# Attention and two MoE layers on one core: the first expert's rows earlier, scatters side by side, new planner prices, another overflow path

## The chip, the cores and the metric

The kernel is one program on one core of a Trainium2 chip. The metric is the device time of one execution in microseconds (us). The engines are TensorE (PE; its weight loads are PEld), VectorE (DVE), ScalarE (ACT), GpSimd (POOL) and SyncE (SP), which here only issues DMAs.

## The reference

Windowed attention with a distance bias on 4 x 8 heads of 576 positions, a dense layer of 2304 tokens through 2048 units, and a layer of eight experts of 1024 units, where each token goes to the expert whose embedding is nearest to it.

```python
scores = scale * q @ k.T + bias            # 128-wide causal window
x = softmax(scores) @ v                    # as 2304 tokens x 512
h = x @ w_in
x = (h - tanh(h)) @ w_out
logits = normed(x) @ normed(expert_emb).T / tau
idx = argmax(logits); gate = softmax(logits)[idx]
for e in range(8):
    mask = idx == e
    out[mask] = gate[mask] * (relu(x[mask] @ w1[e]) @ w2[e])
```

## The kernel before, in words

Tokens run in nine groups of 256 (`NG`), two blocks of 128 each. For a block, `quarter` makes the attention (scores on PE, the bias and the minimum on DVE, the exponential on ACT, a split into high and low parts on ACT and POOL or DVE, a turn by DMA, the product on PE), and `x_out` turns the result into `xT`. For a group, `step` runs eight times (`p` counts steps): the product `h` at L710, tanh on ACT (L715), a subtraction (L718), the high part `gh` (L723, ACT) and the low part `gl` (L727, DVE), and the product `acc` at L734. Every fp32 product is made of three products of such parts. Group 0 is visited twice, with half of the weights each time and group 1 in between.

After its last step `route` takes a group's 256 tokens to the experts: norms, three bfloat16 parts of each row (L806, L810), logits (L819; for the last group L833), the choice (`chain`), the place in the expert's list (`slot`), the gate, and two scatters of 128 rows into `bucket` in DRAM (L890, an indirect DMA of POOL). `emb` makes the normed embeddings `enT` and `en3` (load `ec` at L278, transposes at L293); it borrows the buffers `gh1` and `gl1`. It stands in the loop over visits outside the test for a first visit.

After group 6 `choose` ranks the experts by their counts so far; expert 0 of the second layer is the largest of these. `space` reads the counts again after group 7 and moves that expert's later rows up to row 256 where it has fewer, so that its first two tiles need no row of the last group. `settle` ranks the others after the last group and gives them capacities (`CAPS`, 384 down to 256). `e_rows` fetches a tile of an expert's rows (L1103, a turning DMA, or L1088, a plain one with transposes on PE; `side` at L1108 for gate and token), adds the parts (L1120) and splits the sum into `xA` or `xT` (L1127, L1130). `e_weight` loads weights (L1059, L1061) and splits them (L1065, L1069). `expert` makes `he` (L1169), `ge` (L1185, L1191), `y` (L1200, L1204), scales by the gate (L1225 or L1223) and `put` scatters 128 rows into the output (L1229). The third tile of expert 0 goes through `turned`. At the end `overflow` would take the rows past an expert's capacity: a branch on all engines (L1466) with a loop in it.

The order of all work is made by `Plan.order`: a list of tasks with engines and their costs, due times, what they read and write. It picks the task that can start first, then the one due first. `late` and `lag` are added to the time at which a result counts as there; `port=True` says that the task, on DVE, can't begin while POOL runs; `SW` is POOL's DMA queue. The engines run in the order so made.

## Time and profile before

| | |
|---|---|
| median of 3 runs | 804.57 us (803.22 to 805.38) |
| profiled execution, its own time | 803.59 us |
| its span, first to last instruction | 801.9 us |
| PE busy | 766.4 us (96%) |
| DVE, ACT, POOL busy | 576.8, 424.9, 344.1 us |
| granted TensorE clock, mean | 0.987 |
| moved by DMA | 124.29 MB, 155 GB/s on average |

The profile comes from one execution. Busy time is that of the engine's own instructions; register, branch, semaphore and DMA-issuing instructions don't count. A matmul at a lower granted clock is busy for longer.

### The profile page before, as it was taken

The numbers are of one execution on the slowest core, as the hardware profiler recorded it, in microseconds if no ns is written. First come the engines' busy times: TensorE is split into PE (matmuls) and PEld (weight loads), VectorE is DVE, ScalarE is ACT, GpSimd is POOL, SyncE is SP. The second block draws the span as 40 slices with busy tenths as digits, with TensorE's granted clock in tenths as the row PEclk, the third lists the DMA queues.
The fourth block names the chain that finished last, engine by engine and source line by source line (L and its number), as shares of the span: only waits on it lengthen the run. The fifth ranks groups of instructions, "written<-read, shape, count | busy, mean of one in ns | idle before, by whom it ended". The sixth has DMA issues, their size and how long they took to land.

```text
span 801.9 us, 15261 instructions
## 1 busy us (share of the span) xinstructions
PE 766.4 (96%) x5193; PEld 678.1 (85%) x5193; DVE 576.8 (72%) x1501; ACT 424.9 (53%) x963; POOL 344.1 (43%) x339
## 2 busy tenths in 40 slices
PE   6998999799999999999999999998999999979995
PEld 4877899689898999989989998987889889869894
DVE  4798898688687687698887875978449877657420
ACT  4776876545665464555645642654145655545220
POOL 3233225765564155253644721655124644632210
PEclk9999999899999999999999999999999999999998
DMA  9983389936455264454364425681366988975100
GB/s 322 407 328 112 80 258 281 208 101 135 99 117 143 72 120 101 109 131 115 74 146 113 92 66 125 198 222 42 112 178 198 254 233 214 245 179 175 37 29 30
DMA packets 152472, 124.29 MB, mean 155 GB/s; under 512 B 115309, under 2 KB 119405, under 8 KB 152128
## 3 DMA queue, kind: packets, MB, share of 16 engines
q1 hardware_dynamic: 149360, 111.40, 52.3%
q0 software_dynamic: 3024, 11.82, 4.3%
q8 instruction: 42, 0.69, 0.4%
q14 instruction: 46, 0.38, 0.2%
HBM read 84.30 MB, written 22.06 MB: 133 GB/s over the span
## 4 chain that ended last, share of the span: by engine, by line
PE 74%; DVE 8%; issue 6%; DMA 4%; POOL 3%; ACT 2%; SPq 2%; POOLq 0%; ACTq 0%; DVEq 0%
PE h L710 21%; PE acc L734 20%; PE he L1169 9%; PE y L1204 8%; PE o L571 3%; PE sc L489 3%; PE y L1200 2%; PE of L560 2%; PE sc L483 1%; DMA est<-in_w 1%; SPq L1103 1%; DVE xf L1120 1%; PE misc L546 1%; DMA out<-yo,ix 1%; PE misc L662 1%
## 5 line engine op out<-in xcount | busy, mean ns | idle before, releaser
L710 PE MATMUL h<-xT,wi 128*128 128x256 f32 x1728 | 227.2, 284 | 3.0 <-DVE wi L349 1.6
L710 PEld LDWEIGHTS h<-xT,wi 128*128 128x128 f32 x1728 | 217.7, 191 | 10.1 <-DVE wi L349 2.2
L734 PE MATMUL acc<-wo,gh 128*128 128x512 f32 x576 | 184.9, 402 | 1.2 <-ACT gh L723 1.2
L734 PEld LDWEIGHTS acc<-wo,gh 128*128 128x128 f32 x576 | 101.3, 191 | 17.3 <-ACT gh L723 1.6
L734 PE MATMUL acc<-wo,gl 128*128 128x512 f32 x288 | 113.6, 395 | 0.5 <-DVE gl L727 0.5
L1204 PE MATMUL y<-eo,ge 128*128 128x512 f32 x336 | 88.5, 397 | 4.3 <-DVE ge L1191 2.9
L715 ACT ACTIVATE t<-h 128x512 f32<-128x512 f32 x72 | 43.0, 597 | 84.5 <-PE h L710 83.4
L525 ACT ACTIVATE p<-sc,mx 128x256 f32<-128x256 f32 (+1 forms) x128 | 59.3, 465 | 48.4 <-DVE mx L511 31.5
L1204 PEld LDWEIGHTS y<-eo,ge 128*128 128x128 f32 x336 | 59.6, 188 | 16.3 <-DVE ge L1191 4.7
L511 DVE CUSTOM_DVE_ANT_0 sc<-sc,bias 128x256 f32<-128x256 f32 (+1 forms) x136 | 49.9, 375 | 27.9 <-PE sc L489 19.7
L727 DVE TENSOR_TENSOR gl<-t,gh 128x512 fp32r<-128x512 f32 x72 | 62.3, 866 | 5.7 <-ACT gh L723 4.9
L734 PEld LDWEIGHTS acc<-wo,gl 128*128 128x128 f32 x288 | 54.8, 190 | 13.3 <-DVE gl L727 0.9
L383 POOL TENSOR_TENSOR khl<-stk,khl 64x512 fp32r<-64x512 f32 x25 | 34.4, 1378 | 62.3 <-ACT khl L379 40.8
L1229 POOL DMA_INDIRECT out<-yo,ix x23 | 24.1, 1047 | 86.2 <-ACT yo L1225 57.8
L535 POOL TENSOR_TENSOR ph<-p,ph 128x512 f16<-128x512 f32 (+1 forms) x32 | 38.9, 1216 | 50.8 <-ACT ph L530 35.1
L1191 DVE SCALAR_TENSOR_TENSOR ge<-he,ge 128x256 fp32r<-128x256 f32 x104 | 28.6, 313 | 39.8 <-ACT ge L1185 39.5
L1169 PEld LDWEIGHTS he<-xA,ei 128*128 128x128 f32 x384 | 54.4, 188 | 2.7
L1169 PE MATMUL he<-xA,ei 128*128 128x288 f32 (+2 forms) x384 | 56.5, 295 | 0.0
L1169 PEld LDWEIGHTS he<-xT,ei 128*128 128x128 f32 x384 | 54.5, 192 | 2.2
L1169 PE MATMUL he<-xT,ei 128*128 128x288 f32 (+2 forms) x384 | 55.9, 298 | 0.0
L718 DVE TENSOR_TENSOR t<-h,t 128x512 f32<-128x512 f32 x72 | 49.3, 685 | 7.2 <-ACT t L715 6.9
L723 ACT CAST gh<-t 128x512 fp32r<-128x512 f32 x72 | 44.6, 619 | 16.9 <-DVE t L718 13.3
(223 smaller groups left out, 1416.7 us busy)
## 6 DMA issues: line engine op xcount, KB each, us to landing
est<-in_w SPq DMA_DIRECT2D x128, 256.0 KB
bucket<-in_c_pad SPq DMA_DIRECT2D x8, 1155.0 KB
rawi<-in_w_in SPq DMA_DIRECT2D x16, 511.8 KB
rawo<-in_w_out SPq DMA_DIRECT2D x16, 511.8 KB
stk<-in_k SPq DMA_DIRECT2D x30, 256.0 KB
stq<-in_q SPq DMA_DIRECT2D x28, 256.0 KB
vst<-in_v SPq DMA_DIRECT2D x30, 128.0 KB
xe<-bucket SPq DMA_DIRECT2D x3, 384.0 KB
```

What stands on the lines that cost most here:

```text
L383: self.eng(e).tensor_tensor(out=k, in0=r4("k")[64:128], in1=k.bitcast(F32), op=ALU.subtract)
L511: nc.vector.tensor_tensor_reduce(out=x, in0=x, in1=self.bias[:, h, c0:c1], scale=-0.125, scalar=mx[:, 1:2] if m else 3.0e38, op0=ALU.add, ...
L525: nc.scalar.activation(out=v["p32"][:, jj * W:(jj + 1) * W], in_=x, func=AF.Exp, scale=-1.0, bias=v["mx"][jj][:, 0:1], accum_out=self.sums ...
L535: self.eng(e).tensor_tensor(out=ph[:, 2 * W:4 * W], in0=v["p32"][:, 0:2 * W], in1=ph[:, 0:2 * W], op=ALU.subtract)
L710: nc.tensor.matmul(h3(v["h"], f2), lhsT=w[:, a, k, :], rhs=xT[c][:, :, k, :], start=(k == 0 and n == 0), stop=(k == KD - 1 and n == 2))
L715: nc.scalar.activation(out=v["t"], in_=v["h"].rearrange("p a b -> p (a b)"), func=AF.Tanh)
L718: nc.vector.tensor_tensor(out=v["t"], in0=v["h"].rearrange("p a b -> p (a b)"), in1=v["t"], op=ALU.subtract)
L723: nc.scalar.copy(out=v["gh"], in_=v["t"])
L727: self.eng(e).tensor_tensor(out=v["gl"], in0=v["t"], in1=v["gh"].bitcast(F32), op=ALU.subtract)
L734: nc.tensor.matmul(self.acc[g, t], lhsT=v[a][:, c0:c0 + 128], rhs=self.w["o", fs[f2]][:, c, :], start=(first and f2 == 0 and n == 0), stop ...
L1169: nc.tensor.matmul(h[:, 0:N], lhsT=w[:, a, c0:c0 + 128], rhs=xT()[b][:, k, 0:N], start=(k == 0 and n == 0), stop=(k == KD - 1 and n == 2))
L1204: nc.tensor.matmul(y[t], lhsT=gt(f, a)[:, (t - ts[0]) * 128:(t - ts[0] + 1) * 128], rhs=self.w["o", f0 + f][:, b, :], start=(f == 0 and n ...
```

## The change

- `emb` is called on the first visit of group 0 only.
- `space` runs after group 6, beside `choose`, instead of after group 7. The first two tiles of expert 0 (`soon`) depend on the scatters of groups 0 to 6, and are due ten steps ahead of the expert instead of four.
- The two scatters of a group no longer wait for each other; each follows the two of the group before (the first group's all pads), and the loads of rows follow the last two that were sent. A small memset on POOL stands ahead of the second one. The scatters into the output no longer wait for each other.
- The planner counts the results of the loads of keys, queries, values and expert weights 1.2 us later (`lag=LAG`; one of five places is shown below), takes a scatter to occupy its queue for 1.06 us, and marks some 25 more tasks with `port=True` (three are shown): the low parts of weights, the splits of the probabilities, the row parts, the choice, place, gate and ranking, `keep`, and the sums of the rows.
- The overflow path is written without POOL's DMAs: rows come by SP, and go out through DRAM row by row. A branch hint for POOL is set ahead of it, `nt` holds the counts too.

```diff
+LAG = 1.2
+SOON = 10
...
     def order(self, places):
...
             elif e == "SW":
-                free["POOL"] = max(free.get("POOL", 0.0), st) + 1.04
-                free[e] = st + eng[e]
-                end = st + eng[e] + 2.0
+                free["POOL"] = max(free.get("POOL", 0.0), st) + 1.06
+                free[e] = st + 1.06
+                end = st + eng[e] + 1.5
...
-            lat = self.LAT.get(e, 0.05) + late
+            lat = self.LAT.get(e, 0.05) + late + lag
...
-        self.nt = self.cst.tile([1, 2 * E + 1], I32, name="nt")
+        self.nt = self.cst.tile([1, 3 * E + 1], I32, name="nt")
...
-        P.add(LOENG, lo, due, r=[wf, (key, 0), "at"], w=[(key, 1)])
+        P.add(LOENG, lo, due, r=[wf, (key, 0), "at"], w=[(key, 1)], port=True)
...
-            P.add({"SP": 0.73}, lambda e: load("k"), due - 2, r=["at"], w=[k, "stk"])
+            P.add({"SP": 0.73}, lambda e: load("k"), due - 2, r=["at"], w=[k, "stk"], lag=LAG)
...
         def scatter(t):
-            nc.gpsimd.indirect_dma_start(
+            if t:
+                nc.gpsimd.memset(r["sm"][:, 0, 7:8], 0.0)
+            x = nc.gpsimd.indirect_dma_start(
                 out=self.bucket, out_offset=bass.IndirectOffsetOnAxis(ap=r["ix"][:, t:t + 1].bitcast(U32), axis=0),
-                in_=self.xrow[t], in_offset=None)
+                in_=self.xrow[t], in_offset=None).ins
+            if t:
+                self.tc.declare_no_dep(x, self.sent[-1], reason="each row of the bucket is written once")
+            n = 2 if g != N0 else len(self.sent) - t
+            self.follow(x, self.sent[len(self.sent) - t - n:len(self.sent) - t])
+            self.sent.append(x)
...
-                  r=["ix", "x2g"] + [("x3", t, n) for n in range(3)] + [("pad", n) for n in range(E)], w=["bucket"])
-        P.add({"DVE": 0.4}, cums, due, r=["oh", "small"], w=["cum"])
+                  r=["ix", "x2g"] + [("x3", t, n) for n in range(3)] + [("pad", n) for n in range(E)], w=[("bk", g, t)])
+        P.add({"DVE": 0.4}, cums, due, r=["oh", "small"], w=["cum"], port=True)
+
+    def follow(self, x, insts):
+
+        info = mybir.DependencyInfo(mybir.DependencyClass.Sync, mybir.DependencyReason.DATA)
+        for y in insts:
+            self.tc.add_manual_dep(x, y.name, info, reason="rows of the bucket")
...
-            nc.sync.dma_start_transpose(out=x.rearrange("p n k t -> p (n k) t")[:, :, 0:w], in_=rows)
+            self.follow(nc.sync.dma_start_transpose(out=x.rearrange("p n k t -> p (n k) t")[:, :, 0:w], in_=rows).ins, self.sent[-2:])
...
+        rows = [("bk", g, n) for g in range(NG - 2 if v["soon"] else NG) for n in range(2)]
...
-            P.add({"SP": 2.2}, turn, due - 6, r=["at", "bucket", ("place", c)], w=[x], late=LATE)
+            P.add({"SP": 2.2}, turn, due - 6, r=["at", ("place", c)] + rows, w=[x], late=LATE)
...
-        P.add(add, lambda e: join(e, 1), due, r=[x], w=["xf"])
+        P.add(add, lambda e: join(e, 1), due, r=[x], w=["xf"], port=True)
...
         def put(_, t):
             n = T if short(t) else 128
-            nc.gpsimd.indirect_dma_start(
+            x = nc.gpsimd.indirect_dma_start(
                 out=self.out, out_offset=bass.IndirectOffsetOnAxis(ap=v["ix", t][0:n].bitcast(U32), axis=0),
-                in_=v["yo", t][0:n], in_offset=None, bounds_check=NT - 1, oob_is_err=False)
+                in_=v["yo", t][0:n], in_offset=None, bounds_check=NT - 1, oob_is_err=False).ins
+            for y in self.puts:
+                self.tc.declare_no_dep(x, y, reason="each row of the result is written once")
+            self.puts.append(x)
...
-                if b == 0:
-                    self.emb(P, 0)
+                    if b == 0:
+                        self.emb(P, 0)
...
                 if g == NG - 3:
                     self.choose(P, p + 2)
+                    self.space(P, p + 2)
...
-                self.e_rows(P, v, t, d - 4 + t)
+                self.e_rows(P, v, t, d - (SOON if n == 0 else 4) + t)
             self.expert(P, v, d, n == len(passes) - 1, n == 1)
             if n == 0:
-                self.space(P, due - 6)
                 tail()
...
     def overflow(self):
...
-        load = lambda j: nc.values_load(self.nt[0:1, j:j + 1], min_val=0, max_val=self.NOV * (E if j == E else 1))
-        with tc.If(load(E) > 0):
+        load = lambda j, lo, hi: nc.values_load(self.nt[0:1, j:j + 1], min_val=lo, max_val=hi)
+        tc.mark_branch_hint_location("over", engines=[mybir.EngineType.Pool])
+        with tc.If(load(E, 0, self.NOV * E) > 0, label="over"):
...
+                    nc.sync.dma_start(out=self.bucket[bass.ds(end + e * NT, 128), :], in_=pad)
...
-    def overflow_tile(self, p, e, n, w1, w2, slot, pad, cap):
+    def overflow_tile(self, p, e, n, w1, w2, left, cap):
...
-        nc.gpsimd.indirect_dma_start(
-            out=self.bucket, out_offset=bass.IndirectOffsetOnAxis(ap=ix[:, 0:1].bitcast(U32), axis=0),
-            in_=pad, in_offset=None, bounds_check=ROWS - 1, oob_is_err=False)
-        nc.gpsimd.dma_start(out=x, in_=self.bucket[bass.ds(n * 128 + cap + e * NT, 128), :])
...
+        rows = self.bucket[bass.ds(n * 128 + cap + e * NT, 128), :]
+        nc.sync.dma_start(out=x, in_=rows)
...
-        nc.gpsimd.indirect_dma_start(
-            out=self.out, out_offset=bass.IndirectOffsetOnAxis(ap=ix[:, 1:2].bitcast(U32), axis=0),
-            in_=yo, in_offset=None, bounds_check=NT - 1, oob_is_err=False)
+        nc.sync.dma_start(out=self.pa[0], in_=yo)
+        m = nc.values_load(some, min_val=1, max_val=128)
+        with tc.For_i(0, m) as r:
+            t = nc.sync.value_load(ix[0:1, bass.ds(r, 1)], min_val=0, max_val=NT - 1)
+            nc.sync.dma_start(out=self.out[bass.ds(t, 1), :], in_=self.pa[0][bass.ds(r, 1), :])
```

## Rows read from the trace of the kernel before

**Rows 1.** The page: the span, and each engine's busy time.

```profile
span 801.9 us, 15261 instructions
PE 766.4 (96%) x5193; PEld 678.1 (85%) x5193; DVE 576.8 (72%) x1501; ACT 424.9 (53%) x963; POOL 344.1 (43%) x339
```

**Rows 2.** Busy time by stretch: length, engines in us (instructions), granted clock, DMA.

```profile
300.00:400.00 100.00, 99.65 (x745) 90.00 (x744) 80.45 (x243) 57.12 (x141) 47.81 (x45) 1.00 0.45 107
...
145.70:150.60 4.90, 1.38 (x16) 1.03 (x13) 3.82 (x10) 3.05 (x8) 4.60 (x5) 0.96 0.77 209
150.60:157.40 6.80, 5.58 (x32) 4.28 (x33) 2.83 (x11) 4.73 (x12) 5.01 (x5) 0.53 1.01 227
...
543.30:550.00 6.70, 5.04 (x16) 3.56 (x16) 5.90 (x6) 3.15 (x6) 4.51 (x4) 0.75 0.14 49
550.00:556.50 6.50, 5.91 (x44) 5.03 (x43) 5.66 (x12) 3.59 (x8) 5.25 (x4) 1.00 0.00 0
...
708.70:715.70 7.00, 4.14 (x22) 3.27 (x22) 7.00 (x11) 4.91 (x10) 5.45 (x4) 1.00 0.48 153
715.70:720.60 4.90, 4.72 (x18) 4.02 (x19) 2.97 (x10) 1.90 (x4) 1.35 (x1) 0.65 1.15 202
792.20:801.90 9.70, 0.00 (x0) 0.00 (x0) 0.00 (x0) 0.69 (x1) 0.98 (x1) 0.66 0.09 31
```

**Rows 3.** Waits of PE: who was waited for, us in total, times, longest.

```profile
PE y L1204 <- DVE ge L1191: 2.9, 1, 2.9
PE misc L293 <- DVE ec L288: 2.2, 1, 2.2
...
PE acc L734 <- ACT gh L723: 1.2, 1, 1.2
...
PE acc L734 <- DVE gl L727: 0.5, 1, 0.5
```

**Rows 4.** Timeline of ACT near 146 us: start, length, instruction, idle before it.

```profile
145.67 0.62 ACT L379 CAST khl<-stk 128x512 fp32r<-128x512 f32 x1 [2.77 <-DMA stk<-in_k]
```

**Rows 5.** Timelines of SP, POOL and ACT and two pieces of the chain, 480 to 545.

```profile
494.30 0.38 SPq L1059 DMA_DIRECT2D est<-in_w  x1
...
481.42 1.01 POOL L890 DMA_INDIRECT bucket<-xrow,ix  x1 [0.15 <-issue]
...
528.76 5.11 DMA bucket<-xrow,ix
...
533.89 1.62 SPq L1103
...
543.37 0.62 ACT L1127 CAST xA<-xf 128x512 fp32r<-128x512 f32 x1 [0.21 <-POOL xf L1120]
```

**Rows 6.** Waits of POOL and PE for scatters and the third tile.

```profile
POOL bucket L890 <- DMA bucket<-xrow,ix: 5.9, 4, 2.3
...
PE ht L1286 <- ACT xA L1127: 0.7, 1, 0.7
```

**Rows 7.** Line L727 (ns, least, median, most) and the timeline of DVE.

```profile
L727 DVE TENSOR_TENSOR gl<-t,gh x72: 678/693/1857, 41.0 to 545.1; 128x512 fp32r<-128x512 f32 x72
...
712.29 1.77 DVE L1120 TENSOR_TENSOR xf<-xf,xe 128x512 f32<-128x512 f32 x1
```

**Rows 8.** The tail: timeline, landing of L1229, and the instructions of L1466 and L1579.

```profile
793.24 0.98 POOL L1229 DMA_INDIRECT out<-yo,ix  x1 [4.45 <-ACT yo L1225]
...
DMA to landing us min/median/max: 2.2/3.4/6.5
...
L1466 POOLq EVENT_SEMAPHORE  x5: 17/43/43, 796.2 to 796.5; - x5
...
L1466 POOLq COMPARE_BRANCH  x1: 57/57/57, 793.6 to 793.6; - x1
L1466 POOLq INC_SWDGE_SEM  x1: 995/995/995, 796.6 to 796.6; - x1
...
L1579 POOLq DRAIN  x1: 3426/3426/3426, 797.7 to 797.7; - x1
```

More of the change, by code (lines that the diff above doesn't have):

```diff
@@ L85, in __init__, with add @@
         self.tasks, self.writer, self.readers = [], {}, {}
-    def add(self, eng, fn, due, r=(), w=(), take=None, free=None, late=0.0, port=False):
+    def add(self, eng, fn, due, r=(), w=(), take=None, free=None, late=0.0, port=False, lag=0.0):
         n = len(self.tasks)
@@ L103, in add @@
             self.readers[k] = set()
-        self.tasks.append((eng, fn, due, deps, take, free, late, port))
+        self.tasks.append((eng, fn, due, deps, take, free, late, port, lag))
     def order(self, places):
@@ L128, in order @@
             for n in cand:
-                eng, fn, due, _, take, _, _, port = T[n]
+                eng, fn, due, _, take, _, _, port, _ = T[n]
                 r0 = ready[n]
@@ L146, in order @@
             (st, _, _), n, e = best
-            eng, fn, _, _, take, rel, late, _ = T[n]
+            eng, fn, _, _, take, rel, late, _, lag = T[n]
             if take:
@@ L401, in qk_half @@
             q, qn = ("q", b, hf), ("q", n)
-            P.add({"SP": 0.73}, lambda e: load("q"), due - 2, r=["at"], w=[q, "stq"])
+            P.add({"SP": 0.73}, lambda e: load("q"), due - 2, r=["at"], w=[q, "stq"], lag=LAG)
             P.add({"ACT": 0.65}, qcopy, due, r=["at", q, "stq"], w=[qn])
@@ L444, in v_half @@
         sub = {"DVE": 0.44, "POOL": 0.71}
-        P.add({"SP": 0.36}, load, due - 2, r=["at"], w=[("vst", n)])
+        P.add({"SP": 0.36}, load, due - 2, r=["at"], w=[("vst", n)], lag=LAG)
         P.add({"ACT": 0.44}, lambda e: nc.scalar.copy(out=v[0], in_=st["v"]), due, r=["at", ("vst", n)],
@@ L648, in quarter @@
             P.add({"DVE": 0.42}, recip, due, r=["at"], w=sm, port=True)
-            P.add({"DVE": 0.45, "POOL": 0.66}, mul, due, r=["at"] + sm, w=half)
+            P.add({"DVE": 0.45, "POOL": 0.66}, mul, due, r=["at"] + sm, w=half, port=True)
     def x_out(self, P, b, s, due):
@@ L963, in choose @@
         self.ranking(P, due, 0)
-        P.add({"DVE": 0.8}, pick, due, r=["rank"], w=["big", "first"])
+        P.add({"DVE": 0.8}, pick, due, r=["rank"], w=["big", "first"], port=True)
     def keys(self):
@@ L1029, in settle @@
         self.ranking(P, due, 1)
[L1030 removed]
+        P.add({"DVE": 1.3}, fix, due + 1, r=["rank"], w=["cap", "key2"], port=True)
         P.add({"DVE": 0.2}, least, due + 1, w=["cap"])
@@ L1069, in lo @@
             self.eng(eng).tensor_tensor(out=t[:, 1, :], in0=v["x"], in1=t[:, 0, :].bitcast(F32), op=ALU.subtract)
-        P.add({"SP": 0.73}, load, due - 4, r=["at", ("place", e)], w=[st])
+        P.add({"SP": 0.73}, load, due - 4, r=["at", ("place", e)], w=[st], lag=LAG)
         P.add({"ACT": 0.65}, hi, due, r=[st], w=[(key, 0), (key, 1)])
-        P.add({"DVE": 0.72, "POOL": 1.32}, lo, due, r=[st, (key, 0)], w=[(key, 1)])
+        P.add({"DVE": 0.72, "POOL": 1.32}, lo, due, r=[st, (key, 0)], w=[(key, 1)], port=True)
     def e_rows(self, P, v, t, due):
@@ L1087, in load @@
             rows = self.bucket[bass.ds(self.at_row[c][2] + t * 128, w), :].bitcast(BF16)[:, 0:2 * XW]
-            nc.sync.dma_start(out=u["x"][0:w, :], in_=rows)
+            self.follow(nc.sync.dma_start(out=u["x"][0:w, :], in_=rows).ins, self.sent[-2:])
         def tr(_):
@@ L1107, in side @@
             for p0 in range(0, 128, w):
-                nc.sync.dma_start(out=s[p0:p0 + w, :], in_=self.bucket[bass.ds(self.at_row[c][2] + t * 128, w), XW:ROW])
+                x = self.bucket[bass.ds(self.at_row[c][2] + t * 128, w), XW:ROW]
+                self.follow(nc.sync.dma_start(out=s[p0:p0 + w, :], in_=x).ins, self.sent[-2:])
         def keep(_):
@@ L1469, in overflow @@
             for e in range(E):
-                n = load(e)
+                n = load(e, 0, self.NOV)
                 with tc.If(n > 0):
@@ L1484, in overflow_tile @@
         NF = FE // 128
-        sm = p.tile([128, 2], F32, tag="osm", name="osm")
-        ix = p.tile([128, 2], I32, tag="oix2", name="oix2")
+        some = p.tile([1, 1], I32, tag="osm", name="osm")
+        row = p.tile([1, 128], F32, tag="orow", name="orow")
+        ix = p.tile([1, 128], I32, tag="oix2", name="oix2")
         x = p.tile([128, ROW], F32, tag="ox", name="ox")
-        nc.vector.tensor_tensor(out=sm[:, 0:1], in0=slot, in1=self.cnt[:, e:e + 1], op=ALU.is_lt)
-        nc.vector.tensor_scalar(out=sm[:, 0:1], in0=sm[:, 0:1], scalar1=32768.0, scalar2=float(e * NT),
-                                op0=ALU.mult, op1=ALU.add)
@@ L1499, in overflow_tile @@
-        nc.vector.tensor_scalar(out=slot, in0=slot, scalar1=128.0, scalar2=None, op0=ALU.add)
+        rows = self.bucket[bass.ds(n * 128 + cap + e * NT, 128), :]
+        nc.sync.dma_start(out=x, in_=rows)
+        nc.sync.dma_start(out=row, in_=rows[:, XW + 1:XW + 2].rearrange("r o -> o r"))
+        nc.vector.tensor_copy(out=ix, in_=row)
+        nc.vector.tensor_scalar(out=row[:, 0:1], in0=left, scalar1=128.0, scalar2=None, op0=ALU.min)
+        nc.vector.tensor_copy(out=some, in_=row[:, 0:1])
@@ L1500, in overflow_tile @@
+        nc.vector.tensor_scalar(out=left, in0=left, scalar1=-128.0, scalar2=None, op0=ALU.add)
         xt = p.tile([128, 512], F32, tag="oxt", name="oxt")
```

56 lines of the change are left out of this document (28 added, 28 removed).

## The prediction

> **What bounds the kernel now.** I read the page first: TensorE (PE) is busy 766.4 of 801.9 us [rows 1], so 35.5 us are all that waiting can cost it, plus what it loses where its clock is granted at the lower level. No other engine comes near. So I ask only where PE stands still or slow, which the table of stretches answers [rows 2]. The reader should see five numbers in it. From 145.7 to 157.4 us PE idles 4.90 - 1.38 and 6.80 - 5.58, 4.7 us together, and the granted clock of 0.53 in the second part (half of the time at 1.2 GHz after the idle time before it) costs another 0.47 x 5.58 = 2.6: 7.3 us. From 543.3 to 556.5, the seam between the first MoE and the second, it is 1.66 + 0.59 idle and 0.25 x 6.7 = 1.7 of clock: 3.9. From 708.7 to 720.6 it is 2.86 + 0.18 idle and 0.35 x 4.72 = 1.65 of clock: 4.7. From 792.2 on PE has no work at all: a tail of 9.7. And 300 to 400 shows how full the long middle is: 0.35 idle in 100. The other 16 of the 35.5 are spread over smaller pauses, which I leave as they are. The waits of PE then say who ended each pause [rows 3].
>
> **The embeddings, turned once.** The transposes of the embeddings at L293 run twice, since group 0 is visited twice. The second time PE waits 2.2 us for `ec` [rows 3], right at 146 us. The edit removes that pass: one load, four DVE operations on `ec`, one POOL power, four transposes, one evacuation, five small POOL operations, and the claim on the buffers `gh1` and `gl1`, for which ScalarE's `gh` cast stands behind. At least the 2.2 us go. At most the whole 7.3 of the stretch go, clock included. It need not be all: in the same place ScalarE sits 2.77 us on a load of keys that lands late [rows 4], and the exponentials queued behind it are what PE wants next. The change also tells the planner that such loads land 1.2 us later (LAG), so that it should put the exponentials ahead of that cast. The two edits act on one pause; I take 5.0 of 7.3, nearer the top because the slow clock comes only after the pause.
>
> **The first expert's rows.** In the kernel before, the rows wait for the scatters of group 7: the second is issued at 528.76 and lands 5.11 later, SP then turns the rows at 533.89, the sums follow on DVE and POOL, and the cast of `xA` runs on ScalarE at 543.37 [rows 5]. The cast of `gh` stands behind it, and PE waits 1.2 for `gh` and 0.5 for `gl` [rows 3]. After the change `space` runs after group 6, so tiles 0 and 1 of the first expert need only scatters up to group 6; the last of these is issued at 481.42 [rows 5], and the buffers are open by 494.30, when the first expert weight is loaded. From the reference's inputs I counted the routes: the largest expert has 272 tokens after seven groups, more than the 256 rows, so no gap arises; in the end it has 337 of 384, and no expert passes its capacity, so the overflow path stays untaken. All that moves: two transposes and two side loads on SP (up to 1.62 us each for the transposes), four sums, two casts, two subtractions, and `space`'s three DVE operations. On SP they pass the expert weights' loads, which lose about 4 us against a first use at 550, more than 50 us off: hidden. On DVE and ScalarE they fall into 500 to 530, where the step's own tanh chain comes first in the plan. Without that cover they bring the seam's pause forward and nothing is won. Gain: 1.7 (the two waits) to 3.9 (the whole seam); I take 3.4, the two waits and the 1.7 of clock, and leave the 0.59 after 550, which belongs to the last group's routing and stays. Late next is that routing.
>
> **Scatters side by side.** POOL waits for the first scatter of a group before it sends the second, 5.9 us in four of the nine groups, 2.3 the longest [rows 6]. Without that the rows for tile 2 come about 2.3 us earlier. PE waits 0.7 there, for ScalarE [rows 6], which has other work ahead: 0 to 0.9, taken 0.5. Nine added memsets on POOL, bounded by 0 and 0.98 us each (the put's row in the last group, far off), are hidden by POOL's idle 57%. The output scatters lose their waits too; each is hidden but the last, which waits only for its own data.
>
> **The planner's new prices.** More DVE operations are declared to wait for POOL. The trace bears out that they do: a subtraction at L727 takes 693 ns at the median and 1857 at most [rows 7], and at 712.29 a sum of the same width takes 1.77. The Trainium skill says the same of the cause (SBUF — State Buffer, "SBUF: two separate sides"): VectorE with two SBUF inputs and GpSimd exclude each other for a whole instruction, but an operation with one SBUF input outside a fast mode is not locked. By this rule some newly marked ones (those that read PSUM) are priced too high, and the planner would win less there; the sum would be up to 2.0 less. The pause at 712, where PE waits 2.9 for `ge` [rows 3] behind two such long DVE operations, can lose all 4.7 or stay, and a new pause may arise elsewhere: -7.3 to +4.7. I take +2.0.
>
> **The tail.** The last put is issued at 793.24. POOL's branch over the overflow path is at 793.6, but its next instruction runs at 796.2; then INC_SWDGE_SEM takes 1.0 to 797.6, and a DRAIN 3.43, from 797.7 to 801.1, with 0.8 behind it [rows 8]. The change hints that branch for POOL and takes every POOL DMA out of the branch's body, so the increment that stands in for them should go. If POOL runs straight on when the put's 0.98 are over (794.2), the DRAIN ends at 797.7 and the span 3.4 earlier. If the DRAIN is short, the put's own landing sets the end (3.4 at the median, to 796.6 [rows 8]); with the 0.8 behind the DRAIN counted twice, an estimate for SP's last waits too, that is 798.2 and a gain of 3.7. If the fetch or the landing still holds POOL to 796.6, only the increment's 1.0 is saved. I take 3.4: no row shows anything but the branch between 793.6 and 796.2. The Trainium skill (Runtime: NRT & Kernel Launch, "Instruction fetch mechanics") says that a taken branch whose target isn't near forces a fetch before execution goes on. The rows agree with 2.6 us. The page knows no hint; by it the 2.6 would stay, and that is the third case.
>
> **Sum.** 3.4 + 5.0 + 3.4 + 0.5 + 2.0 = 14.3. From the profiled execution's own 803.59 that is 789.3; the median of the runs is 0.98 above it, so 790.3.
>
> **Rivals.**
> Fetch stays: the tail gives 1.0 instead of 3.4, 792.7. For it: no row shows a hint at work. Against: it is put at the very engine whose branch costs. Chance 0.12.
> The gains are given back: the rows' work, moved to 500 to 530, makes `gh` or `gl` late there, and the key loads, not the embeddings, hold the pause at 146. Left are the tail and 2.2: 803.59 - 5.6 + 0.98 = 799.0. For it: DVE's contention [rows 7] and ScalarE's 2.77 [rows 4]. Against: PE idles hardly at all in the full steps [rows 2]. Chance 0.20.
> All pauses go: 3.7 + 7.3 + 3.9 + 0.9 + 4.7 = 20.5, giving 784.1. For it: each pause has one late instruction ahead of it. Chance 0.12.
> A new pause (the other side): every task between 200 and 500 is ordered anew, and one late exponential there costs PE what 145.7 to 157.4 cost, 7.3 with the clock. With the gains at their lower ends (1.0 + 2.2 + 1.7 = 4.9) one pause gives 807.0; at the likeliest gains it takes two. For it: PE's margin there is thin, 0.35 in 100 [rows 2], because nothing is late now. Against: the new prices are nearer to the rows. Chance 0.10.
>
> **How the numbers follow.** The forecast has 0.46. A kernel like this is told apart from no change from 0.3% on, 2.4 us. Faster come the forecast, the fetch rival, the third rival and most of the second: 0.46 + 0.12 + 0.12 + 0.15 = 0.85; the other 0.05 of the second end within 0.3%; slower 0.10. The range runs from 783 (all pauses gone, a us to spare) to 801 (the gains given back, with two more lost); it leaves out the new pause and little else.
>
> **What would show it.** Right: one `ec` load only; PE full from 145 to 157; `xA` of tiles 0 and 1 cast well before 540 and no wait for `gh` at the seam; no INC_SWDGE_SEM, and POOL's DRAIN starting before 795. Wrong: a fresh stretch below full clock in 100 to 500, the row transposes waiting on SP, or a DRAIN that still ends at 3.4 after SP's last wait.

## The result, and the profile after

The changed kernel takes 784.38 us (median of 4 runs, 783.51 to 785.27), the kernel before on the same chip 803.89 (4 runs, 802.87 to 805.38): ratio 0.9756, 95% interval 0.9734 to 0.9778. The forecast was 790.3, with a range of 783 to 801. By the medians 19.5 us are gained. The profiled execution took 785.27, its span 783.4: 18.5 us less than the span of [rows 1].

The page of the changed kernel, span and busy time:

```profile
span 783.4 us, 15248 instructions
...
PE 760.1 (97%) x5189; PEld 678.7 (87%) x5189; DVE 549.5 (70%) x1454; ACT 427.9 (55%) x969; POOL 382.6 (49%) x378
```

PE's work is the same but for four products (5189); the gain is idle time and clock. VectorE is busy 27 us less than in [rows 1] and GpSimd 39 us more. The table of stretches of the changed kernel, columns as in [rows 2]:

```profile
138.00:162.00 24.00, 23.13 (x178) 19.81 (x177) 20.24 (x52) 15.22 (x39) 16.12 (x16) 1.00 0.94 213
200.00:500.00 300.00, 300.00 (x2256) 272.93 (x2254) 222.90 (x659) 163.35 (x400) 151.62 (x156) 1.00 0.49 112
520.00:530.00 10.00, 7.60 (x43) 6.92 (x44) 8.08 (x20) 4.85 (x10) 7.28 (x6) 0.83 0.41 140
535.00:560.00 25.00, 25.00 (x169) 22.68 (x169) 16.68 (x44) 10.16 (x21) 11.93 (x11) 1.00 0.18 58
680.00:725.00 45.00, 44.77 (x259) 39.86 (x259) 27.68 (x68) 24.11 (x48) 24.55 (x21) 1.00 0.83 225
```

The three stretches that cost most before are full or nearly so: near 146 us, at the seam (535 to 560) and near 710. The largest new pause is in 520 to 530, where PE works 7.60 of 10 us at a clock of 0.83. The waits of PE in the changed kernel name it, and a second one for `p` (2.7, at 65.5 us):

```profile
PE misc L862 <- DVE oh L852: 3.6, 1, 3.6
PE sc L491 <- ACT p L527: 3.1, 3, 2.7
...
PE ht L1306 <- ACT xA L1143: 0.7, 1, 0.7
```

None of the four waits of [rows 3] is left. The wait of [rows 6] for the third tile of turned rows is what it was, 0.7. To see where the 18.5 us came from I put the same piece of PE's work side by side in the two timelines (a step has 24 products `h`; they are L710, in the changed kernel L712):

| the same work of PE | before, us | after, us | gained so far | what lies between |
|---|---|---|---|---|
| first `h` of the 15th step | 139.0 | 139.5 | -0.5 | another start, with the pause at 65.5 |
| first `h` of the 28th step | 239.8 | 232.9 | 6.8 | the pause near 146 is gone, and small ones: 7.3 |
| first `h` of the 70th step | 526.4 | 517.2 | 9.1 | small pauses: 2.3 |
| first `h` of the 71st step | 532.0 | 528.4 | 3.6 | the new pause: -5.5 |
| first `he` of the second expert | 592.9 | 584.8 | 8.1 | the seam: 4.5 |
| PE's last product ends | 792.2 | 776.4 | 15.8 | the pauses of 680 to 725 (7.5) and small ones: 7.7 |
| end of the span | 801.9 | 783.4 | 18.5 | the tail, 9.7 to 7.0: 2.7 |

The tail of the changed kernel, first the timeline of POOL:

```profile
777.38 0.98 POOL L1246 DMA_INDIRECT out<-yo,ix  x1 [4.40 <-ACT yo L1242]
```

then the instructions of the branch over the overflow path (L1489) and of the program's end (L1603), in ns least/median/most, and their first and last start:

```profile
L1489 POOLq COMPARE_BRANCH  x1: 68/68/68, 777.7 to 777.7; - x1
L1489 POOLq EVENT_SEMAPHORE  x1: 17/17/17, 778.2 to 778.2; - x1
...
L1603 POOLq DRAIN  x3: 40/115/4231, 778.3 to 783.1; - x3
```

and the landing of that last put (L1246, from 777 us on):

```profile
DMA to landing us min/median/max: 3.4/3.4/3.4
```

Between the branch and the next instruction 0.5 us pass, where it was 2.6 [rows 8]; there is no INC_SWDGE_SEM; but the long DRAIN takes 4.23 us instead of 3.43. It ends at 782.5, 1.7 us after the put has landed (777.4 + 3.4).

### The profile page after: what moved, and what is told of

Read it like the earlier page. It is cut to its first block, busy times and chain, and to the rows that moved or that the text cites. A ratio compares the mean times of both kernels' runs of the same rounds, so it can differ in the third digit from the quotient of the medians.

```text
span 783.4 us, 15248 instructions
## 1 busy us (share of the span) xinstructions
PE 760.1 (97%) x5189; PEld 678.7 (87%) x5189; DVE 549.5 (70%) x1454; ACT 427.9 (55%) x969; POOL 382.6 (49%) x378
## 4 chain that ended last, share of the span: by engine, by line
PE 87%; DVE 4%; issue 4%; ACT 2%; POOL 2%; DMA 1%; SPq 0%; POOLq 0%
PE h L712 25%; PE acc L736 23%; PE he L1186 12%; PE y L1221 10%; PE o L573 3%; PE sc L491 3%; PE y L1217 3%; PE of L562 2%; PE sc L485 1%; PE misc L548 1%; PE misc L664 1%; PE ht L1306 1%; DMA tmp<-in_c_bias 1%; PE misc L821 1%; DVE xA L1146 0%
## 5 line engine op out<-in xcount | busy, mean ns | idle before, releaser
L712 PE MATMUL h<-xT,wi 128*128 128x256 f32 x1728 | 227.8, 286 | 0.8 <-DVE xT L672 0.5
L712 PEld LDWEIGHTS h<-xT,wi 128*128 128x128 f32 x1728 | 219.7, 193 | 6.8 <-DVE xT L672 0.7
L729 DVE TENSOR_TENSOR gl<-t,gh 128x512 fp32r<-128x512 f32 x72 | 64.4, 895 | 6.7 <-ACT gh L725 6.4
L537 POOL TENSOR_TENSOR ph<-p,ph 128x512 f16<-128x512 f32 (+1 forms) x37 | 43.9, 1187 | 51.1 <-ACT ph L532 40.5
L385 POOL TENSOR_TENSOR khl<-stk,khl 64x512 fp32r<-64x512 f32 x24 | 31.8, 1325 | 67.3 <-ACT khl L381 61.3
L720 DVE TENSOR_TENSOR t<-h,t 128x512 f32<-128x512 f32 x72 | 49.5, 687 | 18.5 <-ACT t L717 18.2
L1246 POOL DMA_INDIRECT out<-yo,ix x23 | 25.0, 1089 | 69.9 <-ACT yo L1242 63.0
L1202 ACT ACTIVATE ge<-he 128x288 fp32r<-128x288 f32 (+2 forms) x56 | 23.2, 414 | 61.2 <-PE he L1186 42.5
```

The lines of the kernel that those rows point to most:

```text
L385: self.eng(e).tensor_tensor(out=k, in0=r4("k")[64:128], in1=k.bitcast(F32), op=ALU.subtract)
L537: self.eng(e).tensor_tensor(out=ph[:, 2 * W:4 * W], in0=v["p32"][:, 0:2 * W], in1=ph[:, 0:2 * W], op=ALU.subtract)
L712: nc.tensor.matmul(h3(v["h"], f2), lhsT=w[:, a, k, :], rhs=xT[c][:, :, k, :], start=(k == 0 and n == 0), stop=(k == KD - 1 and n == 2))
L720: nc.vector.tensor_tensor(out=v["t"], in0=v["h"].rearrange("p a b -> p (a b)"), in1=v["t"], op=ALU.subtract)
L729: self.eng(e).tensor_tensor(out=v["gl"], in0=v["t"], in1=v["gh"].bitcast(F32), op=ALU.subtract)
```

## The experiments

Two theories stood at the start. The first is the prediction's: each edit removes the pause that stands where it was made, so the parts can be put in and taken out one by one and add up. The second: the order of the instructions, planned anew with each price, decides which pauses there are, so a part's worth depends on the others. I put parts alone into the kernel before, took parts out of the changed kernel, and at last went after the new pause. Differences between two variants of the changed kernel are taken from their ratios to the kernel before, times 804 us; each has an uncertainty of some 2 to 4 us.

### Parts put alone into the kernel before

**emb_silent.** The second pass over the embeddings keeps its place in the plan and issues nothing.

```diff
+        silent = hasattr(self, "emb_done")
+        self.emb_done = True
+        do = lambda f: (lambda e: None) if silent else f
...
-        P.add({"SP": 0.2}, load, due, r=[("xT", 0)], w=ec)
-        P.add({"DVE": 0.6}, sq, due, w=["ess"] + ec)
+        P.add({"SP": 0.2}, do(load), due, r=[("xT", 0)], w=ec)
+        P.add({"DVE": 0.6}, do(sq), due, w=["ess"] + ec)
...
```

> The kernel before, in its own order, with the second embedding pass issuing nothing (the first stays, so nothing of the result changes). Theory E (the second pass makes the pause at 146): the 2.2 us wait of TensorE for ec goes, and with it the slow clock behind it; 5 to 7 us less than before, about 797 to 799. Theory K (the late keys' load makes it): ScalarE still sits on that load and the exponentials come late all the same; 1 to 2.6 us less, about 801 to 803, with a pause and a stretch below full clock still standing near 150.

Measured: 804.81 us against 803.29, ratio 1.0019 (1.0002 to 1.0036): nothing gained, less than either theory asked for. The timelines of PE and ACT in this kernel:

```profile
147.94 0.50 PE L492 MATMUL sc<-khl,qst 128*128 128x256 f32 x2 [1.58 <-ACT p L528]
150.91 0.80 PE L492 MATMUL sc<-khl,qst 128*128 128x256 f32 x2 [1.83 <-ACT p L528]
...
143.51 0.62 ACT L382 CAST khl<-stk 128x512 fp32r<-128x512 f32 x1 [1.57 <-DMA stk<-in_k]
147.32 0.47 ACT L528 ACTIVATE p<-sc,mx 128x256 f32<-128x256 f32 x1 [0.17 <-POOL xr L607]
```

PE no longer waits for `ec`, but stands in the same place for the exponentials `p`, which run at 147.3, behind the late cast of keys and what else is queued on ACT. The wait for `ec` was one of several that ended at about the same time: in 138 to 162 PE idles 4.1 us at a clock of 0.86, in the kernel before 4.9 at 0.86. In the changed kernel, where this pause is gone, the exponentials still run behind the cast of the late keys; the timeline of ACT there:

```profile
146.28 0.62 ACT L381 CAST khl<-stk 128x512 fp32r<-128x512 f32 x1 [0.93 <-DMA stk<-in_k]
...
148.70 0.47 ACT L527 ACTIVATE p<-sc,mx 128x256 f32<-128x256 f32 x1 [0.69 <-DVE xr L606]
```

What differs is PE's order: from 144.3 to 150.4 it has accumulations, `o` and `h` products to do, and asks for these `p` only behind them.

**before_lag.** Only the later loads: 1.2 us of lateness on the loads of keys, queries, values and expert weights.

```diff
+LAG = 1.2
...
-            P.add({"SP": 0.73}, lambda e: load("k"), due - 2, r=["at"], w=[k, "stk"])
+            P.add({"SP": 0.73}, lambda e: load("k"), due - 2, r=["at"], w=[k, "stk"], lag=LAG)
...
-        P.add({"SP": 0.73}, load, due - 4, r=["at", ("place", e)], w=[st])
+        P.add({"SP": 0.73}, load, due - 4, r=["at", ("place", e)], w=[st], lag=LAG)
```

> The kernel before with the 1.2 us LAG on the loads of keys, queries, values and expert weights in the planner, both embedding passes kept. Theory E: the pause at 146 stays, as ec is still waited for; within 2 us of before there. Theory K: ScalarE's exponentials now stand ahead of the cast of the late keys, the pause at 146 shrinks by half or more, 3 to 5 us less. For the stretch 703 to 720 (third pause of before): if late weight loads in the plan made it, it goes here (4 to 7 us less); if the port prices did, it stays.

Measured: 802.83 us, ratio 0.9974 (0.9955 to 0.9993), 2.1 us gained, 0.6 to 3.6 by the interval. The pauses in 140 to 155 only move (1.83 at 138.7, 1.68 for `ec` at 143.3), those near 700 are others (1.96 and 1.58), and elsewhere 2.16 at 208.6 and 2.63 at 540.6 come in, as the second theory has it.

**before_rows.** Only the first expert's rows ahead: its space after group 6, its first two tiles tied to the scatters up to group 6.

```diff
+SOON = 10
...
-                  r=["ix", "x2g"] + [("x3", t, n) for n in range(3)] + [("pad", n) for n in range(E)], w=["bucket"])
+                  r=["ix", "x2g"] + [("x3", t, n) for n in range(3)] + [("pad", n) for n in range(E)], w=["bucket"] + ([("bucket", 6)] if g < NG - 2 else []))
...
+        rows = [("bucket", 6)] if v["soon"] else ["bucket"]
...
+                    self.space(P, p + 2)
...
-                self.e_rows(P, v, t, d - 4 + t)
+                self.e_rows(P, v, t, d - (SOON if n == 0 else 4) + t)
```

> The kernel before with only this of the change: the space of the first expert's rows is fixed after group 6 and its first two tiles depend on the scatters up to group 6, so that their load can start ahead of group 7's scatters. No later loads, no price for the port. Theory (the early rows are worth the same by themselves as undoing them costs the changed kernel, 7.2 us, or at least the 3.4 of the prediction): 797 to 800 us, and no wait for the turned rows at the start of the first expert. Rival (without the new prices the order gives it back elsewhere): 802 to 806 us, with pauses over 2 us in places where the kernel before had none.

Measured: 804.79 us against 803.88, ratio 1.0006 (0.9992 to 1.0020): the rival. The rows are early (`xA` is cast by 514.96) and no wait for them is left at the seam. Yet the timeline of PE in this kernel shows other pauses:

```profile
530.41 0.18 PE L861 MATMUL misc<-oh,tri 128*128 128x8 bf16 x1 [1.12 <-DVE oh L851]
...
540.03 0.50 PE L735 MATMUL acc<-wo,gl 128*128 128x512 f32 x1 [1.40 <-DVE gl L728]
```

and a third of 1.53 us at 576.5, where the third tile's rows wait for the last scatters; in 560 to 585 the granted clock is 0.88, where it was 1.00 before. So the seam's wait was taken away and given back in three pieces around it. (The 7.2 of the expectation is the plain difference of two medians; by the ratios it is 6.3.)

### Parts taken out of the changed kernel

**after_emb2.** The embeddings turned twice again.

```diff
-                    if b == 0:
-                        self.emb(P, 0)
+                if b == 0:
+                    self.emb(P, 0)
```

> The changed kernel with the embeddings turned twice again, all planned anew. Theory plan (the pause at 146 is one of order on ScalarE and TensorE, not of the second pass): no pause over 2.5 us near 146, 784 to 787. Theory E in its weak form (in the plan the second pass is what crowds that place): the pause comes back, 790 to 793.

Measured: 784.53 us, ratio 0.9746 (0.9716 to 0.9777), no different from the changed kernel's. Two pauses stand near 148 (1.17 for `ec`, 0.92), and the new pause at 519 is 2.06 instead of 3.58: what the pass costs in its place, the order gives back elsewhere.

**after_lag0.** The loads counted on as before.

```diff
-LAG = 1.2
+LAG = 0.0
```

> The changed kernel with LAG 0. Theory lag: consumers of late loads stand too early again, pauses of 2 to 7 us come back near 146 and near 710; 790 to 797. Theory port: the new port prices carry both places, 783 to 787.

Measured: 789.48 us, ratio 0.9805 (0.9775 to 0.9836), 3.9 us lost. Near 146 no pause comes back. At 519 PE waits 3.94 for `oh`, and near 711 a pause for `ge` stands again; the timeline of this kernel, all engines:

```profile
713.34 0.16 DVE L1130 CAST ix<-side 128x1 int32<-128x1 f32 x1 [6.15 <-DMA out<-yo,ix]
...
713.88 2.07 PE L1221 MATMUL y<-eo,ge 128*128 128x512 f32 x4 [2.83 <-DVE ge L1208]
```

It looks like the pause of 2.9 for `ge` in [rows 3], but it is another one. There VectorE was busy for the whole 7.00 us of 708.7 to 715.7 [rows 2], with two long operations ahead of `ge`; here it stands idle for 6.15 us with the copy `ix` at its head, until a put issued at 705.28 has landed (713.32), and `ge` follows at 713.41. So this run doesn't show that the later loads took the old pause away; it shows a new order with a pause of its own, and its time lies between the two theories.

**after_noport.** The 20 newly declared waits for the port between VectorE and GpSimd taken out (20 places in the code are all that the change adds, not some 25); two of them:

```diff
-        P.add(LOENG, lo, due, r=[wf, (key, 0), "at"], w=[(key, 1)], port=True)
+        P.add(LOENG, lo, due, r=[wf, (key, 0), "at"], w=[(key, 1)])
...
-        P.add({"DVE": 1.35}, chain, due, r=["con", "small"], w=[("lg", 0), ("lg", 1), "oh"], port=True)
+        P.add({"DVE": 1.35}, chain, due, r=["con", "small"], w=[("lg", 0), ("lg", 1), "oh"])
...
```

> The changed kernel without the 20 new port marks; LAG, rows, scatters and tail as changed. Theory port: the pause near 710 (TensorE behind two long DVE operations) comes back, 4 to 7 us, and with it small ones; 789 to 795. Theory lag: 783 to 787. The pause of 3.6 us at 519, which stands behind routing operations locked out by POOL, should not shrink under either.

Measured: 788.72 us, ratio 0.9817 (0.9776 to 0.9858), 4.9 us lost. The page's line of busy times, then the table of stretches of this kernel:

```profile
PE 763.0 (97%) x5189; PEld 676.9 (86%) x5189; DVE 575.0 (73%) x1488; ACT 424.4 (54%) x964; POOL 345.8 (44%) x349
```

```profile
138.00:162.00 24.00, 19.29 (x136) 15.37 (x134) 19.08 (x65) 12.14 (x31) 14.47 (x15) 0.87 0.83 192
505.00:530.00 25.00, 24.87 (x184) 22.34 (x183) 23.01 (x40) 14.71 (x29) 19.61 (x15) 1.00 0.66 198
```

In the stretch near 146 there are pauses again (clock 0.87), but others: 1.84 at 140 for `p`, and 2.31 at 156 for `oh` of a routing chain. The pause at 710 that was to come back stays away; 1.66 for `ge` at 681 is what stands in 680 to 725. The pause at 519, which I had put down to a price still missing, is gone, with fewer prices. That speaks for the second theory. What the marks do by themselves the busy times show: with them VectorE is busy 540 to 554 us and GpSimd 378 to 394 in all eight profiled kernels that have them, without them 575 to 581 us and 340 to 346 in all six that don't. The planner gives the marked work to GpSimd instead.

**after_rowslate.** The first expert's rows tied to group 7 and fixed after it, as before.

```diff
-SOON = 10
+SOON = 4
...
-        rows = [("bk", g, n) for g in range(NG - 2 if v["soon"] else NG) for n in range(2)]
+        rows = [("bk", g, n) for g in range(NG - 1 if v["soon"] else NG) for n in range(2)]
...
-                    self.space(P, p + 2)
...
+                self.space(P, due - 6)
```

> The changed kernel with the first expert's rows tied to the scatters up to group 7 again, space after group 7, and due four steps ahead; all else as changed. Theory rows: the seam's waits for gh and gl and its slow clock come back, 3 to 4 us, while the pause at 519 (which the moved rows may have helped to make) shrinks by 0 to 5; 783 to 788. Rival (the new prices had mended the seam by themselves): no wait over 0.5 us at the seam, and 780 to 784.

Measured: 791.59 us, ratio 0.9834 (0.9800 to 0.9868), 6.3 us lost, more than either theory said. PE's timeline at the seam of this kernel:

```profile
544.39 0.38 PE L1186 MATMUL he<-xA,ei 128*128 128x256 f32 x1 [2.82 <-ACT xA L1143]
```

In 535 to 560 PE works 19.41 of 25 us at a clock of 0.86, against 25.00 at 1.00. A pause of 2.38 for `oh` stays at 513 (3.58 at 519 in the changed kernel), so the moved rows can have added to it but don't make it alone.

**after_serial.** The waits between the scatters of a group, and between all puts, left in.

```diff
-                self.tc.declare_no_dep(x, self.sent[-1], reason="each row of the bucket is written once")
...
-            for y in self.puts:
-                self.tc.declare_no_dep(x, y, reason="each row of the result is written once")
```

> The changed kernel in its own order, but with the waits between the scatters of a group, and between the last puts, left in as before (the declarations that they do not depend on each other are taken out). Theory (the scatters side by side are worth next to nothing, since the first expert's rows are fixed ahead): 783.5 to 785.5 us. Rival (GpSimd, held by each landing, is late with the turned pass and with routing): 786 to 790 us, with TensorE idle behind GpSimd's work.

Measured: 814.30 us, ratio 1.0113 (1.0073 to 1.0152), slower than the kernel before: 28.7 us lost. Both theories were far off. The waits of POOL in this kernel (us in total, times, longest), then one timeline of it over all engines:

```profile
POOL bucket L894 <- DMA bucket<-xrow,ix: 19.5, 7, 4.6
...
POOL out L1244 <- DMA out<-yo,ix: 11.6, 3, 5.4
```

```profile
664.62 0.91 POOL L1244 DMA_INDIRECT out<-yo,ix  x1 [5.40 <-DMA out<-yo,ix]
665.55 1.17 POOL L1134 TENSOR_TENSOR xf<-xe 128x512 f32<-128x512 bf16 x1
...
666.75 2.95 DVE L1134 TENSOR_TENSOR xf<-xf,xe 128x512 f32<-128x512 f32 x1 [9.24 <-POOL xf L1134]
...
670.09 1.22 PE L1219 MATMUL y<-eo,ge 128*128 128x512 f32 x2 [7.96 <-DVE ge L1206]
```

Read it downward: the third put of an expert is held 5.40 us for the landing of the second; the sum `xf` of the next expert's rows stands behind it on POOL; VectorE waits 9.24 for that sum, with `ge` queued behind, and PE 7.96 for `ge`. PE loses nothing up to the first expert: its first `he` runs at 538.1, in the changed kernel at 539.6 (at the 15th step this run is 1.4 ahead). From there to PE's end (804.8 against 776.4) it loses 29.9: 7.5 by the second expert's first `he` (590.8 against 584.8), where the last group's scatters and the first puts run, the rest in the experts behind. The kernel before has such waits too, POOL's 9.9 us for a put to land, in five waits of at most 2.6. PE idles there 5.3 us in all from 590 to 792, so they cost it no more than that and its slow clock: its order has other work between the puts. The timelines of POOL, first of the kernel before, then of the changed one:

```profile
682.52 1.28 POOL L1229 DMA_INDIRECT out<-yo,ix  x1 [0.15 <-issue]
...
687.56 1.00 POOL L1229 DMA_INDIRECT out<-yo,ix  x1 [1.59 <-DMA out<-yo,ix]
...
692.77 1.38 POOL L1229 DMA_INDIRECT out<-yo,ix  x1 [2.88 <-DVE ix L1114]
```

```profile
701.83 1.00 POOL L1246 DMA_INDIRECT out<-yo,ix  x1 [0.87 <-DVE yo L1240]
703.13 1.19 POOL L1246 DMA_INDIRECT out<-yo,ix  x1 [0.30 <-DVE yo L1233]
704.62 1.82 POOL L1246 DMA_INDIRECT out<-yo,ix  x1 [0.30 <-DVE ei L1084]
```

The changed order sends the three puts of an expert one right behind the other. It can, because nothing waits; with the waits put back the same order is ruinous. How the 28.7 divide between scatters and puts beyond this reading of the trace was not measured: no run has one of them alone, and none has the kernel before without these waits.

### The tail, its two edits apart

**before_hint** has only the hint for POOL's branch, **after_nohint** the whole change but the hint (one profiled run each; the tail is read from the end of PE's work to the end of the span).

```diff
+        tc.mark_branch_hint_location("over", engines=[mybir.EngineType.Pool])
-        with tc.If(load(E) > 0):
+        with tc.If(load(E) > 0, label="over"):
```

> The kernel before with the branch hint alone: the overflow body and the increment that stands in for its POOL DMAs stay. Theory: the gap of 2.6 us behind POOL's branch goes; the increment (1.0 us) then ends before the output has landed, so the tail is 7 to 7.5 instead of 9.7. Rival (the increment holds the tail, by making the DRAIN longer): 8.5 to 9.

> The changed kernel without the branch hint, order of work the same. Theory fetch-hint: POOL's next instruction after the branch comes 2.5 us later again, but it now stands beside the output's landing; the tail from TensorE's last matmul (7.0 us in the changed kernel) becomes 7.0 to 7.5. Rival: the hint is what the tail gained, and the tail is 9 or more.

Instructions of POOL's queue at the branch (L1467) and the end (L1580) with the hint alone:

```profile
L1467 POOLq EVENT_SEMAPHORE  x5: 17/43/43, 796.3 to 796.7; - x5
...
L1467 POOLq COMPARE_BRANCH  x1: 68/68/68, 795.8 to 795.8; - x1
L1467 POOLq INC_SWDGE_SEM  x1: 1007/1007/1007, 798.7 to 798.7; - x1
...
L1580 POOLq DRAIN  x3: 40/109/3426, 799.7 to 803.7; - x3
```

and without the hint in the changed kernel (L1488, L1602):

```profile
L1488 POOLq COMPARE_BRANCH  x1: 57/57/57, 774.1 to 774.1; - x1
L1488 POOLq EVENT_SEMAPHORE  x1: 17/17/17, 776.7 to 776.7; - x1
...
L1602 POOLq DRAIN  x3: 40/107/3426, 776.8 to 780.8; - x3
```

and the landing of the last put with the hint alone (L1229, issued at 795.48):

```profile
DMA to landing us min/median/max: 3.2/3.2/3.2
```

The hint does what it says: 0.5 us from the branch to the next instruction with it, 2.6 without. But alone it is worth 0.2 (the tail is 9.5 instead of 9.7), because INC_SWDGE_SEM then begins only at 798.7, when that put lands. The increment's removal alone is worth 1.4 (a tail of 8.4), both together 2.7. Neither of the expected tails came, in either run. Executions differ here as much as some of these parts: the old tail is 9.7, 9.8, 10.0 and 10.6 us in the kernel before, before_lag, before_rows and emb_silent, the new one 7.0 in the changed kernel and 6.5 to 6.8 in seven variants of it. By the middle of the two groups it gained 3.3, and the 0.2 of the hint is no more than their spread.

### The new pause

The timeline of the changed kernel, all engines, at 519:

```profile
518.58 1.27 POOL L1084 TENSOR_TENSOR ei<-est,ei 128x512 fp32r<-128x512 f32 x1 [0.68 <-ACT ei L1080]
518.64 1.24 DVE L848 TENSOR_TENSOR eq<-lg,rs 128x16 f32<-128x16 f32 x1
519.81 2.51 POOL L1084 TENSOR_TENSOR eo<-est,eo 128x512 fp32r<-128x512 f32 x2
519.91 1.19 DVE L849 TENSOR_TENSOR lg<-lg,rs 128x16 f32<-128x16 f32 x1
...
521.43 0.92 DVE L852 TENSOR_TENSOR oh<-con,rs 128x16 bf16<-128x16 f32 x1
...
522.40 0.18 PE L862 MATMUL misc<-oh,tri 128*128 128x8 bf16 x1 [3.58 <-DVE oh L852]
```

The routing chain of group 7 is a row of small VectorE operations on 16 columns. Four of them take 0.9 to 1.3 us (three are shown; the first, L830, took 1.31 from 516.62 on), each ending where a subtraction of expert weights on POOL ends. PE stands ahead of the position matmul L862 with twelve `h` products and the accumulation queued behind it. So I told the planner that this one chain is 3.0 us later.

**after_late_pos.**

```diff
-        P.add({"DVE": 1.35}, chain, due, r=["con", "small"], w=[("lg", 0), ("lg", 1), "oh"], port=True)
+        P.add({"DVE": 1.35}, chain, due, r=["con", "small"], w=[("lg", 0), ("lg", 1), "oh"], port=True, lag=3.0 if g == NG - 2 else 0.0)
```

> The changed kernel with one more lateness: the routing chain of group 7 is counted on 3.0 us later, so that its position matmul stands behind the next twelve h matmuls and part of the accumulation in TensorE's order; everything ahead of it is in the same order as in the changed kernel. Theory: TensorE's pause near 519 us (3.6 us idle before the position matmul, and some 1.5 us of lower clock behind it) goes, and nothing takes its place: 779 to 780.5 us, ratio to the kernel before about 0.970. Rival: the lateness only moves the pause to the slot, the scatters or the first expert's rows, or the order behind it gets worse: 783 to 787 us, with a pause of over 2 us elsewhere between 515 and 560.

Measured: 779.49 us (779.47 to 781.61, 5 runs), ratio 0.9699 (0.9681 to 0.9716), 4.6 us less than the changed kernel: the theory. The timeline of this kernel:

```profile
517.41 1.30 POOL L1084 TENSOR_TENSOR ei<-est,ei 128x512 fp32r<-128x512 f32 x1 [0.21 <-ACT ei L1080]
...
518.78 0.17 DVE L849 TENSOR_TENSOR lg<-lg,rs 128x16 f32<-128x16 f32 x1
...
519.09 3.08 POOL L1084 TENSOR_TENSOR eo<-est,eo 128x512 fp32r<-128x512 f32 x2 [0.38 <-ACT eo L1080]
...
519.28 1.14 DVE L852 TENSOR_TENSOR oh<-con,rs 128x16 bf16<-128x16 f32 x1
...
522.11 0.18 PE L862 MATMUL misc<-oh,tri 128*128 128x8 bf16 x1
```

PE has other work until `oh` is there; 0.79 us of the pause is left, for `gl`, and the clock stays at 1.00 in 505 to 530. The operation L849 takes 0.17 us here, in a gap between two of POOL's subtractions, and 1.19 in the changed kernel beside one.

**after_late_all.** The same lateness for the chain of every group but the last.

```diff
+        P.add({"DVE": 1.35}, chain, due, r=["con", "small"], w=[("lg", 0), ("lg", 1), "oh"], port=True, lag=3.0 if g < NG - 1 else 0.0)
```

> The changed kernel with the routing chain of every group but the last counted on 3.0 us later, so that the whole order is planned anew. Theory (a chain's lateness is what the planner lacks): the pauses before position matmuls go everywhere, 779 to 782 us. Rival (a new order has as many pauses as another, only in other places): 783 to 790 us.

Measured: 784.67 us, ratio 0.9750 (0.9731 to 0.9769): the rival. The wait for `oh` shrinks to 0.76, but the whole order is another one, with new pauses: 1.21 at 211.3 for `gl` and 1.80 at 538.7 for `t`, where the clock falls to 0.93 in 535 to 560. A better price in all places is not a better order.

## Why the prediction was right, and where not

The sign and the bound (PE's pauses and their clock) came out: 14.3 us forecast, 18.5 gained. So did the signs that were to show it: one load of `ec`, PE full from 145 to 157, `xA` cast by 508, no INC_SWDGE_SEM, POOL's DRAIN beginning right behind the put. That the sum came so near is in part luck: the way there differs in nearly every term, and a new pause of 5.5 that no term has stands against gains that were larger than their terms.

**Readings.** Two numbers of the first step are misread and change little. A mean granted clock of 0.53 between the levels 1.0 (2.4 GHz) and 0.5 (1.2 GHz) means nearly the whole stretch at the lower one, not half of it; the price of 2.6 stays. And the seam's clock is priced over the stretch (0.25 x 6.7 = 1.7) where the other two are priced over PE's busy time; by their rule it is 0.25 x 5.04 = 1.3, and the seam is 3.5 instead of 3.9.

**Embeddings, 5.0.** Nearly the whole 7.3 of the stretch is gone: in 138 to 162 PE idles 0.87 us at a clock of 1.00. But the step gave it to the wrong edits. Alone the removed pass is worth nothing (emb_silent), and put back it costs nothing that can be measured (after_emb2). Nor is it LAG, which was to put the exponentials ahead of the cast: they still run behind it, and without LAG no pause comes back there (after_lag0). Without the port's prices there are pauses in the stretch again, for other tasks (after_noport); whether it was these prices that took the old one away is not shown. The step that failed is that at least the 2.2 us of PE's wait for `ec` go: with that releaser gone, the next one, ACT's `p`, was late by nearly as much.

**First expert's rows, 3.4.** The mechanism held: no wait at the seam, 25.00 of 25 us busy. The term was too small: 4.5 by the table, 6.3 by undoing it. The 0.59 after 550 went too, which the step had left standing. That the rows' work is hidden in 500 to 530 holds at most in the changed order, where the pause at 519 is 1.2 shorter without it (after_rowslate), and not in the old one, where the same edit alone gave 0 (before_rows). Late next was not the last group's routing but that of group 7.

**Scatters, 0.5.** Nothing came where the step looked: the 0.7 before the third tile is still there, waiting on ACT. But "the output scatters lose their waits too; each is hidden but the last" holds at most for the order of the kernel before. In the changed one their waits and the scatters' would together cost 28.7 us. The edit is less a gain than a condition for the rest of it.

**Planner's prices, 2.0.** The term was too small and its place too narrow. Taken out one at a time, the port's prices are worth 4.9 and the later loads 3.9. The pause at 712 went, and with it the others of 680 to 725, 7.5 in all; but neither run brings that pause back, so no run shows which of the prices took it away. What the traces do show is that the port's marks move some 25 to 40 us of work from VectorE, whose long operations made that pause, to GpSimd. The new price of a scatter was not tried alone. The Trainium skill (SBUF — State Buffer, "SBUF: two separate sides") gave the rule by which marks on operations that read PSUM are too dear; no run separates those from the others, so whether they cost anything is open.

**Tail, 3.4.** Measured 2.7 in this pair of executions, 3.3 between the middles of all. The branch and the increment went as forecast, and POOL ran straight on from the put (777.38 + 0.98) into the DRAIN (778.3). The term's mistake is that the DRAIN takes 3.43 wherever it begins: it also outlasts the landing of the put by 1.7, and this put landed late, 3.4 us after its issue, where it took 3.0 to 3.1 in the four variants whose landing the trace has. So the put's landing sets the end, as in the step's second case, though the DRAIN is not short. The Trainium skill (Runtime: NRT & Kernel Launch, "Instruction fetch mechanics") lets a taken branch to a far target wait for a fetch; with the hint the run shows 0.5 us where 2.6 stood.

**The rivals.** The fetch did not stay. The gains were not given back as a whole, nor at `gh`. The measured 784.4 is almost the 784.1 of the third rival, in which all pauses go, but by chance: its pauses went, smaller ones besides, and the new one took 5.5 back. That new pause is smaller than the 7.3 of the fourth rival and stands at 519 instead of 200 to 500, where PE is busy 300.00 of 300 us; at the gains that came it could not decide the sign. In the middle of the kernel the price of a re-planned order was nothing.

## What to carry to other kernels

A wait in the profile names who came last, not who would have come next: before counting it as a gain, look for the other instructions that end within the same microsecond or two. In a kernel whose order comes from a planner, an edit's worth is that of the new order: the waits of scatters and puts, which cost the old order little, cost the new one some 29 us, and an early load that was worth 6 us in one order was worth nothing in the other; so try parts both ways, put in alone and taken out. A pause that comes back in the same place need not be the same pause: read what the engine ahead of it was doing. And when a single late instruction stops TensorE, try the lateness on that one task before giving it to all of its kind: 4.6 us here against 0.

## What the runs showed of the hardware

- INC_SWDGE_SEM, in a branch that is not taken, began when the last put had landed: at 798.7 in before_hint, where POOL's queue was free 2 us earlier (last EVENT_SEMAPHORE at 796.7) and the put, issued at 795.48, took 3.2. Without the hint the first instruction behind the branch also came 0.02 to 0.11 us after the landing in the four executions of the old tail, 2.6 to 3.3 us after the branch; so how much of the 2.6 is the fetch by itself stays open. With the hint it took 0.5 us while the put was still under way.
- POOL's last DRAIN took 3.43 us where it began 3 us or more after the last put was issued (773.74 to 776.8 in after_nohint, 795.48 to 799.7 in before_hint). Where it began right behind the put it took 3.72 to 4.23 and ended 1.7 us after the landing, in all five executions whose landing the trace has: in after_late_pos the put was issued at 772.14 and landed 3.0 later, and the DRAIN ran 3.75 from 773.1.
- Puts sent side by side land later: 4.4 us after their issue at the median in the changed kernel, 3.4 in the kernel before [rows 8], 3.2 with the waits left in (after_serial). A copy into `ix`, which a put reads, can wait for that, as the 6.15 us of after_lag0 show.
- A VectorE operation on 16 columns with two SBUF inputs took 0.17 us alone and up to 1.31 beside a GpSimd subtraction. A row of such operations is slowed more by a busy GpSimd, in proportion, than the wide ones of [rows 7] (693 to 1857 ns).
